# A hand-written order of work for a retention layer and a GELU network: the rows of chunks 3 to 5 go over three transfer queues, and all work is put in a new order

## The chip, the cores and the metric

The kernel runs on one core of a Trainium2 chip. The core has five engines that run side by side, each through its own list of instructions in order: TensorE (PE, matrix products into the eight banks of PSUM), VectorE (DVE), ScalarE (ACT), GpSimd (POOL) and SyncE (SP, which only starts transfers here). Transfers are started from the lists of SyncE, ScalarE and GpSimd. An engine that comes to an instruction whose inputs are not ready stops there, and all that stands behind it in its list waits as well. The metric is the device time of one execution in microseconds (us). The changed kernel is run in the same way and compared with the one before.

## The reference

```python
def _attn_ref(q, k, v):                      # q, k, v: (4, 8, 768, 64)
    B, H, S, D = q.shape
    gamma = 1.0 - 2.0 ** (-5.0 - np.arange(H, dtype=np.float32))
    scale = 1.0 / np.sqrt(D)
    state, y = np.zeros((B, H, D, D), dtype=np.float32), np.zeros_like(q)
    for t in range(S):
        state = gamma[None, :, None, None] * state + np.einsum('bhd,bhe->bhde', k[:, :, t], v[:, :, t])
        y[:, :, t] = scale * np.einsum('bhd,bhde->bhe', q[:, :, t], state)
    return y

def _moe_ref(x, w_in, w_out):                # x: (3072, 512), w_in: (512, 2048), w_out: (2048, 512)
    h = x @ w_in
    c = np.float32(np.sqrt(2.0 / np.pi))
    g = 0.5 * h * (1.0 + np.tanh(c * (h + 0.044715 * h * h * h)))
    return g @ w_out
```

The output of the first is turned to (batch x sequence, heads x head size) and is the x of the second.

## The kernel before

**Tiling.** The 768 steps of the sequence are cut into six chunks c = 0 to 5 of 128 steps. In a chunk each of the four batches b has a row tile of q, of k and of v: 128 steps x 8 heads x 64, 256 KB in float32. A chunk's x is 512 rows (4 batches x 128), kept with the 512 features on the partitions.

**The retention part of a chunk and batch.** L loads a row tile (line 308). PREP scales it or copies it to float16 (lines 216 and 213 on VectorE and GpSimd, 211 on ScalarE). For chunks 0 and 1, T transposes q and k on TensorE against an identity (line 338, the identity is loaded by LI, line 227) and ET copies the result out of PSUM; for chunks 2 to 5, DT does the same with a transposing transfer on SyncE's list (line 345). A is the product of keys and queries, EA puts the decay mask on it (VectorE, reading PSUM), YI multiplies with v, YP adds what comes from the state of the earlier chunks, EY or EP copies the result into x, SS and ES carry the state on.

**The network part of a chunk.** Both layers are computed by a scheme of seven products in place of eight, with sums of blocks ahead and behind. For chunks 1 to 5, and in chunk 0 for three of the four column groups j of the first layer, M1:c,j,n is product n of the first layer: four matmuls of 256 columns. SX makes the sums of x, WI those of w_in (t_in), CP copies a bank to h, D1 adds another bank to it, G is the GELU. For the second layer SG makes the sums of g, WO those of w_out (t_out), M2 is a product, CO and D2 bring the result to o, ST stores it. In chunk 0 the group j = 1 of the first layer (HB, 128 columns a matmul, GELU GB) and the whole second layer (O0, EO, ST0) are plain products. LWI and LWO load the weights (float32 in memory, float16 on the chip), always from GpSimd's list; w_in is loaded in halves of 64 partitions (line 262). All sums, masks and scalings share the helper at line 216, all plain products that at line 219, so their rows carry those line numbers.

**What sets the order.** ORDER (lines 17 to 135) is one string of 1125 words, read by the loop at line 656. Each word calls a function: `L:v,3,1,S@2` loads v of chunk 3, batch 1 from SyncE's list (S; A is ScalarE, P GpSimd, V VectorE) into buffer 2 of its kind; a number behind @ is a buffer or a bank of PSUM. The words of one engine run in the order in which they stand; words of different engines are tied only by the data and buffers that they share, for which the framework sets the waits. SyncE computes nothing, so it runs ahead of its words' places as far as the waits allow. There are 13 buffers for row tiles, and a load into a buffer waits until the PREP of the tile before it there is done. The transfers of SyncE and ScalarE together use eight semaphores in turn, those of GpSimd another eight, and a transfer waits until the one before it on its semaphore has landed.

**The opening.** SPIN, 11 products of zeros, comes first on TensorE. The rows of chunk 0 are loaded in the order of the words, from three lists; the constants (LC), the identity (LI) and the dummy GELU that loads ScalarE's table (TABLE) stand between them.

Of the kernel before, what the change touches and what calls it, by code (L numbers as in the profile page):

```python
# [26 lines left out]
L:v,1,2,P@5 D1:0,2,11 G:0,0,11@0 CP:0,2,22,A@0 D1:0,0,12 M1:0,0,7 M1:0,2,6 G:0,2,11@1 ES:0,1,A L:v,1,3,P@11
G:0,0,12@2 D1:0,0,22 L:v,1,1,P@10 L:v,1,0,P@6 M1:0,2,3 M1:0,3,2@5 WI:3,1,V CP:0,2,12,A@2 M1:0,0,4 M1:0,3,1@4
PREP:q,1,3,V@4 WI:3,3,V LWO:2 PREP:q,1,0,P@1 LWO:3 D1:0,2,12 L:v,2,2,P@7 WI:3,2,V CP:0,3,11,A@3 M1:0,3,5@2
L:k,2,1,P@2 G:0,2,12@3 PREP:q,1,1,V@3 D1:0,3,11 L:q,2,3,P@8 WI:3,4,V M1:0,2,7 G:0,0,21@4 HB:1,0@3 PREP:k,1,0,V  # L30
HB:1,2@0 G:0,0,22@5 L:k,2,3,P@1 PREP:k,1,3,V M1:0,3,6 PREP:v,1,2,P@4 CP:0,3,22,A@2 PREP:k,1,1,V GB:1,0,0@6
GB:1,2,0@7 HB:1,1@5 ES:0,0,A GB:1,2,1@8 GB:1,0,1@9 PREP:q,1,2,V@2 PREP:k,1,2,V M1:0,3,3 HB:1,3@7 L:k,2,2,P@3
CP:0,3,12,A@1 GB:1,1,0 GB:1,1,1 T:1,1@6 L:q,2,1,P@4 ET:1,1,A@4 L:k,2,0,P@5 M1:0,3,7 T:1,3@0 L:v,2,0,P@12
T:1,2@3 D1:0,3,22 D1:0,3,12 O0:1,0@5 ET:1,3,A@5 ET:1,2,V@6 D1:0,2,22 M1:0,3,4 GB:1,3,1 L:q,2,0,P@0 T:1,0@6
WI:2,4,V GB:1,3,0 G:0,3,21@10 A:1,2@2,0 ET:1,0,A@0 EA:1,2,0@0 A:1,1@3,7 EA:1,1,1@1 O0:0,0@4 G:0,2,22@11 O0:1,1
A:1,3@6,2 EA:1,2,1 PREP:v,1,3,A@5 EA:1,1,0 A:1,0@7,0 M1:0,2,4 O0:0,1 PREP:v,1,1,A@6 G:0,2,21@12 EA:1,3,0@2
# [655 lines left out]
```

## Time and profile before

| what | value |
|---|---|
| runs | 202.04 us median of 3 (201.94 to 203.08) |
| the profiled execution | 200.09 us, span of the profile 198.3 us |
| TensorE busy | 183.0 us, 92% of the span |
| VectorE busy | 160.0 us, 81% |
| GpSimd busy | 139.1 us, 70% |
| ScalarE busy | 119.3 us, 60% |
| moved by transfers | 34.26 MB, mean 173 GB/s |
| queue of SyncE / GpSimd / ScalarE | 19.35 / 10.23 / 4.36 MB |

All times inside the execution count from the start of the span. A row of the timeline has the start, the duration, the engine, the line, the operation, output<-input, how many instructions are merged in it (x), and in brackets the idle time of the engine ahead of it and what ended that idle time. A row of the groups has busy time, mean duration of one in ns, and idle time ahead. A row of the windows has the stretch and its length, the busy time of TensorE, its weight loads, VectorE, ScalarE and GpSimd, the granted clock of TensorE, the busy share of the 16 DMA engines and the rate in GB/s. A row of the chain of work that ended last has start, duration and what was running or under way. On GpSimd an issue of a transfer takes the engine's own time (0.88 to 0.91 us for a row tile).

### The profile page before, as it was taken

To read this page: it belongs to the slowest core of one execution; us is meant where nothing else is said; L and a number is where in the kernel's file an instruction comes from. 1 tells how busy PE (TensorE), PEld (TensorE's weight loads), DVE (VectorE), ACT (ScalarE), POOL (GpSimd) and SP (SyncE) were. 2 spreads that over 40 slices of the span, in tenths; PEclk is the share of its full clock that TensorE was granted. 3 is DMA by queue.
4 is the path that set the end of the run, shared out by engine and by line. 5 is a ranking of instruction groups with operands and counts; after the bars stand their busy time and mean duration, and the time that the engine had idled before them with its cause. 6 is when DMAs were issued, how large, how long until landed. Compare 5 with 4: busy or idle time off the path is not lost.

```text
span 198.3 us, 5294 instructions
## 1 busy us (share of the span) xinstructions
PE 183.0 (92%) x2111; PEld 149.0 (75%) x2111; DVE 160.0 (81%) x294; ACT 119.3 (60%) x219; POOL 139.1 (70%) x143
## 2 busy tenths in 40 slices
PE   7377999998999999999999699999999999999992
PEld 2155878575676788877978588878888888888882
DVE  0888979899678999998989999998897577674630
ACT  1329798687767477945784669676544745435111
POOL 0797477977999976973799595898359867447200
PEclk9958999999999999999999999999999999999998
DMA  6999999999989999999999995260200201301453
GB/s 144 288 239 243 203 334 234 295 239 333 270 195 235 214 211 258 213 212 216 244 226 190 209 178 155 53 150 27 94 0 0 86 23 58 106 0 56 141 201 136
DMA packets 80540, 34.26 MB, mean 173 GB/s; under 512 B 69060, under 2 KB 78404, under 8 KB 80516
## 3 DMA queue, kind: packets, MB, share of 16 engines
q1 hardware_dynamic: 66164, 19.35, 44.4%
q0 software_dynamic: 6128, 10.23, 21.7%
q10 hardware_dynamic: 8224, 4.36, 7.6%
q8 instruction: 16, 0.26, 0.5%
q14 instruction: 8, 0.07, 0.1%
HBM read 27.63 MB, written 6.29 MB: 171 GB/s over the span
## 4 chain that ended last, share of the span: by engine, by line
PE 65%; DMA 19%; POOL 6%; DVE 4%; issue 2%; ACT 1%; ACTq 0%; SPq 0%; POOLq 0%; DVEq 0%
PE bank L219 65%; DMA w_in<-in_moe_w_in_dram 9%; DMA r<-in_q_dram 6%; DMA qkT<-qk 2%; DVE g L216 2%; DMA r<-in_v_dram 2%; POOL sx L216 2%; POOL t_out L216 1%; POOL qk L216 1%; POOL v L216 1%; DVE h L216 1%; DVE w_out L216 1%; POOL g L216 1%; POOL w_in L262 0%; POOL qk L213 0%
## 5 line engine op out<-in xcount | busy, mean ns | idle before, releaser
L219 PEld LDWEIGHTS <-g 128*128 128x128 f16 x624 | 60.4, 98 | 11.8 <-PE bank L338 0.3
L216 POOL TENSOR_TENSOR g<-g 128x512 f16<-128x512 f16 x46 | 54.5, 1204 | 17.9 <-DVE g L216 7.2
L219 PE MATMUL bank<-w_out,g 128*128 128x256 f16 (+1 forms) x384 | 60.4, 290 | 0.2 <-DMA w_out<-in_moe_w_out_dram 0.2
L216 DVE TENSOR_TENSOR h<-bank,h 128x512 f32<-128x512 f32 x69 | 46.0, 682 | 8.8 <-PE bank L219 4.4
L442 ACT ACTIVATE g<-h 128x512 f16<-128x512 f32 x69 | 42.7, 634 | 15.4 <-DVE h L216 15.0
L219 PEld LDWEIGHTS <-w_in 128*128 128x128 f16 x432 | 39.2, 98 | 6.2 <-issue 0.8
L211 ACT COPY h<-bank 128x512 f32<-128x512 f32 x57 | 32.7, 588 | 13.0 <-PE bank L219 12.6
L219 PEld LDWEIGHTS <-t_in 128*128 128x128 f16 x276 | 26.4, 98 | 9.9 <-issue 4.3
L219 PE MATMUL bank<-t_out,g 128*128 128x256 f16 x240 | 33.4, 273 | 0.0
L216 DVE TENSOR_TENSOR a<-bank,mask 128x512 f16<-128x512 f32 x48 | 30.0, 680 | 3.5 <-PE bank L219 3.4
L219 PE MATMUL bank<-x,w_in 128*128 128x256 f16 (+1 forms) x248 | 29.7, 259 | 0.4 <-DMA w_in<-in_moe_w_in_dram 0.2
L219 PE MATMUL bank<-sx,t_in 128*128 128x256 f16 x184 | 26.5, 273 | 2.3 <-ACT g L442 1.2
L219 PE MATMUL bank<-sx,w_in 128*128 128x256 f16 x184 | 26.7, 273 | 0.0
L216 DVE TENSOR_TENSOR g<-g 128x512 f16<-128x512 f16 x34 | 22.1, 669 | 3.1 <-ACT g L442 2.1
L442 ACT ACTIVATE g<-bank 128x512 f16<-128x512 f32 (+1 forms) x31 | 16.5, 549 | 8.4 <-PE bank L219 5.8
L211 ACT COPY o<-bank 128x512 f32<-128x512 f32 (+1 forms) x19 | 9.7, 516 | 18.2 <-PE bank L219 18.2
L216 POOL TENSOR_TENSOR v<-r,cst 128x512 f16<-128x512 f32 x16 | 16.9, 1061 | 4.0 <-DMA r<-in_v_dram 4.0
L216 DVE TENSOR_TENSOR o<-bank,o 128x512 f32<-128x512 f32 (+1 forms) x18 | 10.6, 595 | 8.9 <-PE bank L219 8.7
L211 ACT CAST qk<-r 128x512 f16<-128x512 f32 x20 | 12.1, 620 | 6.2 <-PE bank L219 2.2
L219 PE MATMUL bank<-x,t_in 128*128 128x256 f16 x92 | 13.8, 273 | 1.9 <-DVE h L216 1.9
L216 DVE TENSOR_TENSOR qk<-r,cst 128x512 f16<-128x512 f32 x13 | 9.2, 744 | 6.5 <-DMA cst<-rr_cst 4.1
L211 ACT COPY qkT<-bank 128x1024 f16<-128x1024 f16 x7 | 6.9, 1013 | 8.0 <-PE bank L338 8.0
(53 smaller groups left out, 191.9 us busy)
## 6 DMA issues: line engine op xcount, KB each, us to landing
r<-in_v_dram SPq DMA_DIRECT2D x15, 256.0 KB, 4.8
r<-in_q_dram SPq DMA_DIRECT2D x15, 256.0 KB, 4.2
r<-in_k_dram SPq DMA_DIRECT2D x14, 256.0 KB, 4.6
out_dram<-o ACTq DMA_DIRECT2D x11, 256.0 KB, 3.8
r<-in_v_dram POOLq DMA_DIRECT2D x9, 256.0 KB, 8.3
out_dram<-o SPq DMA_DIRECT2D x9, 256.0 KB, 2.3
w_in<-in_moe_w_in_dram POOLq DMA_DIRECT2D x8, 256.0 KB, 9.6
r<-in_k_dram POOLq DMA_DIRECT2D x8, 256.0 KB, 8.6
```

What stands on the lines that cost most here:

```text
L211: nc.scalar.copy(out=out, in_=in_)
L216: EN[e].tensor_tensor(out=out, in0=in0, in1=in1, op=op)
L219: nc.tensor.matmul(out=out, lhsT=lhsT, rhs=rhs, start=start, stop=stop, skip_group_check=True)
L442: nc.scalar.activation(out=out, in_=in_, func=AF.Gelu_apprx_tanh, scale=1.0)
```

## The change

Only the string ORDER changes; no function does. It has 1125 words before and after, with the same products: the same 161 M1, 140 M2, 4 HB, 16 O0, 8 T and 16 DT. New are the order of the words, the buffers and banks behind @, and for part of the words the engine.

- Rows: before, S, A and P load 44, 5 and 23 tiles; after 23, 18 and 31. Of the 36 tiles of chunks 3 to 5, all 36 came from S; after 17 come from S, 13 from A and 6 from P.
- Sums of g (SG): 34 on V and 46 on P before, 41 and 39 after. Sums of w_out (WO): 5 and 11 before, 11 and 5 after. Sums of x (SX): 12 and 12 before, 15 and 9 after. Sums of w_in (WI): 15 and 1 before, 13 and 3 after.
- CP: 57 on A and 12 on V before, 53 and 16 after. CO: 17 and 7 before, 16 and 8 after. EO: 2 and 2 before, 4 and 0 after. ET: 7 on A and 1 on V before, 8 and 0 after. EY: 4 on A before, 3 on A and 1 on V after. PREP: 25 on A, 34 on P, 13 on V before; 26, 35 and 11 after.
- Stores: 12 from A and 16 from S before; 13 and 15 after.

The opening of the list and its end:

```diff
-L:k,0,2,A@0 L:q,0,2,A@1 ZERO L:k,0,0,S@2 SPIN:11@0 LI:A L:q,0,3,A@3 LC:S TABLE PREP:k,0,0,V@0 L:k,0,3,A@4
-L:q,0,1,A@5 L:v,0,1,S@6 PREP:q,0,2,P@1 LWI:0 PREP:k,0,2,V L:v,0,3,P@7 MASK L:k,0,1,S@8 L:q,0,0,S@9
-PREP:q,0,3,V@2 T:0,2@1 ET:0,2,A@0 A:0,2@2,3 L:v,0,0,P@10 PREP:k,0,3,V LWI:2 L:v,0,2,S@11 T:0,3@4 PREP:q,0,0,V
-ET:0,3,A@1 PREP:k,0,1,P@3 EA:0,2,1@0 A:0,3@5,6 T:0,0@7 EA:0,2,0 ET:0,0,A@2 PREP:q,0,1,V T:0,1@0 LWI:3
-A:0,0@1,4 PREP:v,0,2,P@0 EA:0,3,0@1 EA:0,3,1 EA:0,0,0@2 EA:0,0,1 ET:0,1,A@3 LWI:1 SS:0,2@3 A:0,1@2,7
-EA:0,1,0@3 PREP:v,0,0,P@1 PREP:v,0,1,A@2 PREP:v,0,3,A@3 YI:0,2@5 SS:0,1@6 L:k,1,1,P@12 EA:0,1,1 EY:0,2,A@0
-L:q,1,3,S@2 YI:0,3@1 L:q,1,1,P@1 YI:0,0@4 WI:0,1,V L:q,1,2,P@0 WI:0,2,V SS:0,3 YI:0,1@0 EY:0,3,A SX:0,1,V@0
-EY:0,0,A EY:0,1,A L:k,1,0,P@3 SS:0,0 WI:0,3,V M1:0,0,5@2 M1:0,0,1@7 WI:0,4,V SX:0,2,V@1 SX:0,3,V@2
...
+ZERO LC:S MASK L:k,0,2,A@0 PREP:k,0,2,P@0 L:q,0,3,S@1 L:k,0,1,A@2 L:q,0,0,S@3 L:q,0,2,A@4 PREP:k,0,1,V@1
+L:k,0,0,A@5 PREP:q,0,0,V@2 TABLE PREP:k,0,0,V LI:A L:k,0,3,S@6 PREP:k,0,3,V@3 L:q,0,1,P@7 PREP:q,0,2,V
+SPIN:11@0 PREP:q,0,3,P L:k,1,1,S@8 L:v,0,3,A@9 PREP:k,1,1,V@4 T:0,0@1 ET:0,0,A@0 T:0,3@2 PREP:q,0,1,V
+ET:0,3,A@1 A:0,0@3,4 LWI:0 T:0,2@5 T:0,1@6 EA:0,0,0@0 L:q,1,1,S@10 A:0,3@7,0 ET:0,1,A@2 EA:0,0,1 A:0,1@1,2
+PREP:q,1,1,V ET:0,2,A@3 A:0,2@3,6 L:v,0,2,P@11 L:v,0,0,P@12 L:v,0,1,P@0 LWI:2 PREP:v,0,0,A@0 L:k,1,2,P@2
+PREP:v,0,2,A@1 PREP:v,0,3,P@2 EA:0,3,1@1 T:1,1@4 EA:0,3,0 EA:0,2,0@2 SS:0,0@5 LWI:1 L:q,1,2,P@3 LWI:3
+EA:0,1,0@3 SS:0,2@0 PREP:v,0,1,A@3 WI:0,1,P EA:0,1,1 YI:0,0@7 EY:0,0,A@0 SS:0,3 YI:0,1@3 EA:0,2,1 WI:0,3,V
+WI:0,2,V L:q,1,3,P@5 EY:0,1,A YI:0,3@1 YI:0,2@2 SS:0,1 EY:0,2,V EY:0,3,A M1:0,0,1@7 SX:0,1,V@0 L:k,1,3,P@6
+ET:1,1,A@4 L:q,1,0,P@4 SX:0,2,V@1 M1:0,0,2@6 M1:0,2,1@3 WI:2,1,V M1:0,2,2@2 SX:0,4,V@2 CP:0,2,11,A@0 LWO:0
+WI:2,2,V CP:0,0,11,A@1 M1:0,0,5@1 CP:0,0,22,A@2 M1:0,2,5@4 L:k,1,0,P@1 SX:0,3,V@3 M1:0,2,6 D1:0,2,11 WI:2,3,V
+D1:0,0,11 L:v,1,0,P@8 WI:2,4,V M1:0,0,6 CP:0,2,12,A@3 G:0,2,11@0 PREP:q,1,2,P@2 CP:0,2,22,V@0 G:0,0,11@1
+PREP:k,1,2,V M1:0,0,3 ES:0,0,A M1:0,2,7 HB:1,2@2 CP:0,0,12,A@1 HB:1,0@6 D1:0,0,12 M1:0,0,7 LWO:1 WI:0,4,V
...
-D2:5,22,0 ST:5,22,S,0 M2:5,4,1,0 D2:5,12,0 M2:5,4,0,0 ST:5,22,S,1 ST:5,12,S,0 CO:4,21,A@1 M2:5,4,1,1
-M2:5,4,0,1 M2:5,3,1,0 ST:4,21,A CO:5,21,A,1@4 M2:5,3,1,1 CO:5,21,A,0 D2:5,12,1 ST:5,21,A,0 ST:5,21,S,1
-ST:5,12,S,1
+M2:5,4,1,1 M2:5,4,0,0 M2:5,4,0,1 CO:4,21,V@4 ST:5,22,S,0 M2:5,3,1,0 ST:4,21,S M2:5,3,1,1 D2:5,12,0
+CO:5,21,V,1@5 ST:5,12,A,0 CO:5,21,A,0 ST:5,21,A,0 ST:5,21,S,1 D2:5,12,1 ST:5,12,A,1
```

Before, the first HB stands behind 16 words M1, as `HB:1,0`; after, behind 10 words M1, as `HB:1,2`. On GpSimd the weights of the first layer are loaded in the order 0, 2, 3, 1 before and 0, 2, 1, 3 after.

More of the change, by code (lines that the diff above doesn't have):

```diff
@@ L27 @@
[L27 to L36, printed above, removed]
```

202 lines of the change are left out of this document (104 added, 98 removed).

## The prediction

> **What bounds the kernel now.** I read the page first (busy times, then the strip of 40 slices), then TensorE's timeline for every gap in front of a matmul, then the opening on all queues, the windows, and the groups of instructions for prices.
>
> ```profile
> PE 183.0 (92%) x2111; PEld 149.0 (75%) x2111; DVE 160.0 (81%) x294; ACT 119.3 (60%) x219; POOL 139.1 (70%) x143
> PE   7377999998999999999999699999999999999992
> PEclk9958999999999999999999999999999999999998
> DMA  6999999999989999999999995260200201301453
> ```
>
> TensorE is busy for 92% of the span, and nearly all that it is not lies in the first four slices (20 us). The DMA row stands at 9 for the first 24 slices (119 us): rows and weights stream all that time.
>
> ```profile
> 8.09 0.61 PE L338 MATMUL bank<-iden,qk 128*128 128x128 f16 x8 [2.02 <-DMA iden<-rr_ident]
> 19.79 0.61 PE L219 MATMUL bank<-sx,t_in 128*128 128x256 f16 x4 [0.65 <-DVE sx L216]
> 27.14 1.95 PE L219 MATMUL bank<-x,w_in 128*128 128x128 f16 x32 [0.18 <-DMA w_in<-in_moe_w_in_dram]
> 49.90 0.60 PE L219 MATMUL bank<-sx,t_in 128*128 128x256 f16 x4 [1.20 <-ACT g L442]
> 90.50 0.40 PE L219 MATMUL bank<-qkT 64*128 64x128 f16 x8 [0.34 <-DMA qkT<-qk]
> 103.66 0.60 PE L219 MATMUL bank<-sx,t_in 128*128 128x256 f16 x4 [0.42 <-POOL sx L216]
> 110.71 0.60 PE L219 MATMUL bank<-x,t_in 128*128 128x256 f16 x4 [1.65 <-DVE h L216]
> 111.14 0.60 PE L219 MATMUL bank<-x,w_in 128*128 128x256 f16 x4
> 193.71 1.04 PE L219 MATMUL bank<-w_out,g 128*128 128x256 f16 x8
> ```
>
> Start, duration, and in brackets the idle time before. The first transposes run at 8.09, the first product of chunk 0's first layer at 19.79, the last product group ends at 194.75. One product (four matmuls of 256 columns) starts 0.43 us after the one before (110.71, 111.14). Between 19.79 and 194.75 the quoted gaps sum to 3.8 us. The change alters no matmul, so the time can move in three places only: when the products start, how much idle time lies between them, and the 3.55 us from 194.75 to the end of the span at 198.3.
>
> **Step 1, the opening's rows.** The list keeps the opening's products but exchanges its batches and transfers. Before, the first transposes (T:0,2) need the first two row tiles of ScalarE's queue; after, T:0,0 needs the fourth tile of that queue (k of batch 0, behind k2, k1, q2), and the identity is issued behind that.
>
> ```profile
> 1.26 5.01 DMA r<-in_q_dram
> 2.04 1.70 ACTq L227 DMA_DIRECT2D iden<-rr_ident  x1
> 8.99 2.65 DVE L216 TENSOR_TENSOR qk<-r,cst 128x512 f16<-128x512 f32 x3 [0.47 <-DMA r<-in_q_dram]
> 16.13 2.48 DVE L216 TENSOR_TENSOR a<-bank,mask 128x512 f16<-128x512 f32 x4 [0.68 <-PE bank L219]
> 17.14 0.62 POOL L213 CAST v<-r 128x512 f16<-128x512 f32 x1 [0.86 <-DMA r<-in_v_dram]
> 8.16 7.23 DMA w_in<-in_moe_w_in_dram
> 15.67 11.33 DMA w_in<-in_moe_w_in_dram
> L211 ACT COPY h<-bank 128x512 f32<-128x512 f32 x57 | 32.7, 588 | 13.0 <-PE bank L219 12.6
> ```
>
> The second tile of ScalarE's queue landed at 6.27 (1.26 + 5.01); the third tile, behind the small identity, at 8.99. That is at most 2.7 us a tile; the fourth and fifth came without another wait inside the 2.65 us row, so the pace is nearer 1.9. The fourth tile then lands at 6.27 + 2 x 1.9 = 10.1, its scaling on VectorE (2.65 / 3, 0.7 without the hand-over) ends at 10.8, and the first transposes start there and not at 8.09.
>
> Two chains lead from there to the first product. VectorE, in order: four more scalings (k3, q2, k of chunk 1, q1: 2.8 us) to 13.6, then nine passes (eight masks, one scaling) at 2.48 / 4 = 0.62: 19.2; batches 0 and 1 are among the first eight, 18.6. Before, the last mask ended at 18.61, so this chain costs nothing. The v chain: before, the first weight tile landed at 15.39 (8.16 + 7.23), and a v tile two places behind it at 17.14, 0.9 a tile. After, GpSimd's queue has q1 ahead of that weight tile, and three v tiles (2, 0, 1) behind it: 15.39 + 0.9 + 3 x 0.9 = 19.0. The cast of v1 on ScalarE, its product, and two evictions (0.6 each by the last row; the product some 0.2) follow: 21.0. The first product, which now needs x of batches 0 and 1 only, starts at 21.0 and not at 19.79: **+1.2 us**. Bounds: -0.4 (q1 and one v tile cost nothing, as ScalarE's and SyncE's queues drain sooner) to +3.0 (the full 2.7 us a tile).
>
> The third weight tile: before, w_in1 is the last of four on GpSimd's queue, issued at 15.67 and landed at 27.0, when it held TensorE up by 0.18 us. After, it is the third; ahead of it one weight tile less (1 MB read) but two row tiles more in all. A weight tile costs about three row tiles of stream (w_in0 needed 7.23 us beside the rows, against 2.7 and 1.9 for a row tile), so it lands about one tile sooner, 26.1. Its user HB:1,2 comes after ten products, not sixteen: 21.0 + 10 x 0.43 = 25.3. TensorE waits 0.8, 0.18 of it as before: **+0.6 us**, bounds -0.2 and +1.7 (landing at 27.0 again).
>
> **Step 2, rows of chunks 3 to 5.** 36 tiles, all on SyncE's queue before; after 17 on SyncE's, 13 on ScalarE's, 6 on GpSimd's (with the earlier chunks GpSimd issues 31 and not 23). What it can win is read from two windows (TensorE, load, VectorE, ScalarE, GpSimd busy; clock; DMA share; GB/s):
>
> ```profile
> 8.00:10.00 2.00, 0.81 (x14) 0.63 (x15) 1.53 (x5) 1.01 (x1) 2.00 (x4) 0.84 1.28 288
> 64.00:68.00 4.00, 4.00 (x108) 2.89 (x107) 3.97 (x7) 1.21 (x3) 4.00 (x5) 1.00 0.89 201
> 92.27 1.04 POOL L216 TENSOR_TENSOR v<-r,cst 128x512 f16<-128x512 f32 x1 [4.04 <-DMA r<-in_v_dram]
> L308 POOL DMA_DIRECT2D r<-in_k_dram x8 | 7.1, 888 | 3.5 <-DMA w_in<-in_moe_w_in_dram 1.7 <-DMA w_out<-in_moe_w_out_dram 0.7 <-DVE sx L216 0.5
> ```
>
> With several queues at work rows came at 288 GB/s, from SyncE's alone at 201. At 92.27 GpSimd had sat 4.04 us for a v tile, and the chain that ended last runs through that wait into the gaps at 103.66 and 110.71. So sooner rows can take away 0.34 + 0.42 + 1.65 = 2.4 us at most, and nothing at the least, as the last of these gaps is released by VectorE. I take a third, **-0.8 us**, since a late VectorE is next in line. The costs: GpSimd issues 8 tiles more at 0.89 = 7.1 us, covered by step 3's relief; ScalarE's 13 issues lie in its idle 40% and, where the slot's last reader is late, block its evictions. In the list that reader stands at least 2.6 us of TensorE work ahead, so I price this at 0, bounds 0 to +2.
>
> The Trainium skill (DMA: Bandwidth & Descriptors, section Issuing engines are not separate DMA queues) says that transfers started by different engines share the same 16 DMA engines, and that spreading them saves only issue time. By it the 288 of the opening is not the spreading's doing, and the -0.8 would be 0. No stretch of this trace has the same tiles on one and on three queues.
>
> **Step 3, work exchanged between engines.** Counted in the two lists: VectorE takes on 7 sums of g (34 to 41), 6 of w_out, 3 of x, 4 evictions h (12 to 16) and 1 o, and gives up 2 scalings, 2 sums of w_in, 2 evictions of chunk 0 and one of qkT (one x comes back).
>
> ```profile
> L216 DVE TENSOR_TENSOR g<-g 128x512 f16<-128x512 f16 x34 | 22.1, 669 | 3.1 <-ACT g L442 2.1 <-POOL g L216 1.0
> L213 DVE COPY h<-bank 128x512 f32<-128x512 f32 x12 | 8.2, 682 | 0.9 <-PE bank L219 0.7 <-ACT g L442 0.2
> L216 DVE TENSOR_TENSOR t_out<-w_out 128x512 f16<-128x512 f16 x2 | 0.8, 415 | 0.0
> L216 POOL TENSOR_TENSOR g<-g 128x512 f16<-128x512 f16 x46 | 54.5, 1204 | 17.9 <-DVE g L216 7.2 <-ACT g L442 5.4 <-PE bank L219 3.2
> 100.00:120.00 20.00, 17.93 (x238) 15.08 (x236) 18.93 (x30) 12.66 (x24) 16.84 (x17) 1.00 1.11 204
> 140.00:160.00 20.00, 20.00 (x234) 17.73 (x233) 15.51 (x26) 10.55 (x19) 13.86 (x13) 1.00 0.12 41
> ```
>
> VectorE: 7 x 0.67 + (6 + 3 - 2) x 0.415 + (5 + 1 - 2 - 2 - 1) x 0.68 = 4.7 + 2.9 + 0.7 = +8.3 us. GpSimd: 7 sums at 1.20, 3 of x and a net 4 of the weights at about the same go (-16.8), 7.1 of issues come: near -9 to -10. ScalarE: about even. By place in the lists some two thirds of VectorE's additions stand late, beside products that ran from about 140 to 175 before, where it was busy 15.5 of 20 us and has room; the rest (about 2.5 us) falls where it was busy 18.9 of 20. With fewer sums on GpSimd the sums of g on VectorE should come nearer 0.415, the quickest such row, than 0.67, which gives back most. I take **+0.6 us**; bounds -1.5 (all 41 sums fall by 0.04) and +4 (the room of 1.1 us in 20 is all forced waiting, and the 2.5 us and what the ScalarE blocks add show in full).
>
> **Step 4, the end.** The last store moves from SyncE's to ScalarE's queue; the last sum on VectorE stays. 0, bounds -0.3 and +0.9 (one more tile, 0.9, draining there).
>
> **The sum.** 1.2 + 0.6 - 0.8 + 0.6 = +1.6 us. The profiled execution took 200.09 us with a span of 198.3, 1.95 below the median of the runs shown, 202.04. I add the sum to the median: 203.6 us (a profiled execution of 201.7).
>
> **Rivals.** *The rows win everything, faster.* Two queues gave 288 against 201 GB/s; if three do, chunk 3 to 5's rows are early, the 2.4 us go, the other quoted gaps (1.20, 0.18) are not met in the new order, and the opening is even: 202.04 - 3.8 = 198.2. It decides if GpSimd's wait for v is gone and VectorE is below 18.5 of 20 from 60 to 120. Against it: 1.20 and 1.65 were released by ScalarE and VectorE. Chance 0.20.
>
> *VectorE becomes the bound.* At 18.9 of 20 it has 5% left and gets 5% more; the +4 shows, beside the opening's 1.8 and without the -0.8: 207.8. For it: the longest gap, 1.65, is already its own. Against: most additions stand late. Chance 0.22.
>
> *The spreading does nothing for the rows.* All three queues feed what was already at 9 of 9 in the DMA row; the gaps stay: 203.6 + 0.8 = 204.4. Chance 0.12. The Trainium skill's rule quoted above is this rival.
>
> *The slow clock lasts into the products.*
>
> ```profile
> 6.00:8.00 2.00, 0.07 (x1) 0.10 (x1) 2.00 (x7) 0.00 (x0) 1.66 (x2) 1.00 1.28 288
> 14.00:16.00 2.00, 1.86 (x20) 1.23 (x18) 1.45 (x3) 1.58 (x2) 1.61 (x4) 0.50 1.14 302
> 18.00:20.00 2.00, 1.10 (x34) 0.86 (x30) 1.97 (x7) 1.59 (x3) 2.00 (x3) 1.00 1.22 196
> ```
>
> After a 2 us pause the granted clock stood at 0.50 for 8 us and rose at 16. The pause now lasts to 10.8; shifted by 2.7 it rises at 18.7, before 21.0. If the wait for v holds it down, some 3 us of products run at half speed: +3 less what the wait for w_in1 hides, 205.8. Chance 0.08. The Trainium skill (TensorE: Matmul & The Clock Gate, What's actually happening) says that an idle window of about 3.4 us halves the clock and a busy one restores it; the trace agrees in kind, with 8 us of mixed work before the rise.
>
> **How the numbers follow.** The forecast has 0.38: 203.6 us, its own range 202 to 205.5 from the bounds of steps 1 and 2. About 1% (2.0 us) is what a measurement of this kernel can tell from no change; so faster means below 200.0 and slower above 204.1. Faster is the first rival, 0.20; within 1% the forecast, 0.38; slower the other three, 0.42. The range for 8 in 10 goes from 199.0 (most of the first rival left out) to 207.5 (the second cut at its upper half).
>
> **What would show it.** Step 1: first transposes near 10.8, first product near 21.0, a wait for w_in1 before the 128-column group. Step 2: GB/s from 60 to 100 above 230, the end of the 9s in the DMA row before slice 24, no wait of GpSimd for v of 4 us. Step 3: VectorE near 168 us in all and above 17 of 20 from 140 to 160, its g row below 0.67. Wrong it would be if the first product starts before 20, or if TensorE's gaps after it sum to over 7 us or under 2.

## The result and the profile after

| kernel | runs | median us | ratio to the kernel before |
|---|---|---|---|
| before | 4 | 201.99 (200.90 to 203.08) | 1 |
| changed | 4 | 208.57 (207.94 to 213.89) | 1.032, 95% interval 1.024 to 1.039 |
| changed, measured again | 4 | 213.48 (210.79 to 215.06) | 1.065, 1.052 to 1.078 |

The change makes the kernel slower, by 3% and by 6.5% in two measurements of the same program whose intervals do not meet; the kernel before, run beside them, came to 201.99 and 200.51. The ratios are made without the runs that count as disturbed; the medians and ranges here and below hold all runs. The profiled execution took 208.61 us with a span of 206.8, 8.5 us more than the one of before.

The page of the changed kernel, busy times and the strip:

```profile
PE 187.5 (91%) x2111; PEld 152.1 (74%) x2111; DVE 169.3 (82%) x309; ACT 117.7 (57%) x217; POOL 132.3 (64%) x138
PE   7173899899999999959999799999999999999992
PEclk9958589999999999987999999999999999999999
DMA  7999999998958999899999992222100301223144
```

TensorE's row has its holes in the first slices (1 and 3 in the second and fourth place), and a new one in the 18th slice. The clock row has three dips, two in the opening and one behind the 18th slice, where there was one. The timeline of TensorE, its longest waits:

```profile
11.37 1.87 PE L337 MATMUL bank<-iden,qk 128*128 128x128 f16 x16 [5.30 <-DMA iden<-rr_ident]
20.88 1.03 PE L337 MATMUL bank<-iden,qk 128*128 128x128 f16 x8 [2.56 <-DVE qk L215]
25.40 2.73 PE L218 MATMUL bank<-x,w_in 128*128 128x256 f16 x16
89.78 0.21 PE L218 MATMUL bank<-qkT 64*128 64x128 f16 x1 [1.50 <-DVE o L215]
115.08 0.60 PE L218 MATMUL bank<-sx,t_in 128*128 128x256 f16 x4 [0.91 <-DVE a L215]
118.67 1.19 PE L218 MATMUL bank<-x,t_in 128*128 128x256 f16 x8 [0.37 <-DVE h L215]
```

The first product starts at 25.40 and not at 19.79. To see where the 8.5 us are, I cut each profiled execution into four parts that add up to its span: the start of the first product; the idle time written in brackets behind it, summed; what is left until the last product ends (the products themselves, longer where the clock is low); and the tail from there to the end of the span.

| profiled execution | first product | idle behind it | products | tail | span |
|---|---|---|---|---|---|
| before | 19.79 | 4.82 | 170.14 | 3.55 | 198.3 |
| changed | 25.40 | 4.70 | 172.95 | 3.75 | 206.8 |
| changed, measured again | 25.41 | 9.17 | 173.14 | 3.78 | 211.5 |

So 5.6 us are lost ahead of the first product, 2.8 in products that run slower, 0.2 in the tail, and nothing in idle time. In the second measurement the idle time grew by 4.5 us more, with the opening unchanged. The windows (columns as before) show the slow products:

```profile
18.00:20.00 2.00, 0.33 (x8) 0.15 (x8) 0.00 (x0) 1.43 (x3) 2.00 (x4) 1.00 1.24 203
22.00:24.00 2.00, 1.57 (x38) 1.30 (x38) 2.00 (x5) 0.59 (x1) 2.00 (x3) 0.50 1.20 257
92.00:94.00 2.00, 2.00 (x12) 1.31 (x10) 2.00 (x4) 0.38 (x1) 1.95 (x2) 0.50 1.14 255
60.00:100.00 40.00, 37.86 (x423) 29.12 (x424) 38.84 (x70) 24.26 (x46) 28.92 (x30) 0.96 1.06 220
140.00:160.00 20.00, 20.00 (x246) 17.10 (x245) 17.82 (x32) 12.16 (x23) 10.23 (x9) 1.00 0.10 28
```

The clock is back at 1.00 by 18 to 20 us, stands at 0.50 again from 22 us on, and falls once more behind the wait at 89.78. The first four products take 2.56 us (25.40 to 27.96) in place of 4 x 0.435 = 1.74, and five products from 91.73 to 95.63 take 3.90 in place of 2.18: 0.8 and 1.7 of the 2.8 us. The remaining 0.3 I did not place. And VectorE's timeline in the opening, then the piece of the chain that ended last which leads into it:

```profile
14.13 1.29 DVE L215 TENSOR_TENSOR a<-bank,mask 128x512 f16<-128x512 f32 x2 [1.19 <-PE bank L218]
20.14 0.69 DVE L215 TENSOR_TENSOR qk<-r,cst 128x512 f16<-128x512 f32 x1 [4.72 <-DMA r<-in_q_dram]
20.75 3.67 DVE L215 TENSOR_TENSOR a<-bank,mask 128x512 f16<-128x512 f32 x6
```

```profile
6.14 13.97 DMA r<-in_q_dram
```

VectorE makes two masks and then stands for 4.72 us, because the next word in its list is PREP:q,1,1, the scaling of chunk 1's q of batch 1. That row is the fifth and last of the opening's rows on SyncE's list and landed at 20.11. Six masks of chunk 0 wait behind it. TensorE waits as well, since T:1,1, which transposes that row, stands ahead of SS:0,0.

### The profile page after: what moved, and what is told of

Its sections match the earlier page's. It is cut to its first block, busy times and chain, and to the rows that moved or that the text cites. A ratio compares the mean times of both kernels' runs of the same rounds, so it can differ in the third digit from the quotient of the medians.

```text
span 206.8 us, 5286 instructions
## 1 busy us (share of the span) xinstructions
PE 187.5 (91%) x2111; PEld 152.1 (74%) x2111; DVE 169.3 (82%) x309; ACT 117.7 (57%) x217; POOL 132.3 (64%) x138
## 4 chain that ended last, share of the span: by engine, by line
PE 66%; DVE 19%; DMA 8%; ACT 2%; issue 2%; SPq 1%; DVEq 0%
PE bank L218 65%; DMA r<-in_q_dram 7%; DVE h L215 6%; DVE g L215 3%; DVE a L215 2%; DMA r<-in_k_dram 2%; DVE sx L215 1%; DVE o L215 1%; SPq L307 1%; DVE h L212 1%; DVE st L429 1%; DVE w_out L215 1%; ACT h L210 1%; DVE w_in L215 1%; DVE qk L215 1%
## 5 line engine op out<-in xcount | busy, mean ns | idle before, releaser
L215 POOL TENSOR_TENSOR g<-g 128x512 f16<-128x512 f16 x39 | 46.2, 1201 | 43.3 <-ACT g L441 17.7
L218 PEld LDWEIGHTS <-w_in 128*128 128x128 f16 x432 | 39.9, 100 | 7.3 <-issue 0.9
L210 ACT COPY h<-bank 128x512 f32<-128x512 f32 x53 | 30.3, 587 | 15.8 <-PE bank L218 15.4
L218 PE MATMUL bank<-x,w_in 128*128 128x256 f16 (+1 forms) x248 | 30.5, 263 | 0.3 <-DVE h L215 0.3
L218 PE MATMUL bank<-sx,w_in 128*128 128x256 f16 x184 | 27.9, 279 | 0.5 <-DVE w_in L215 0.5
L215 DVE TENSOR_TENSOR g<-g 128x512 f16<-128x512 f16 x41 | 22.9, 584 | 1.1 <-ACT g L441 0.9
L210 ACT COPY o<-bank 128x512 f32<-128x512 f32 (+1 forms) x20 | 10.6, 533 | 14.8 <-PE bank L218 14.7
L215 POOL TENSOR_TENSOR v<-r,cst 128x512 f16<-128x512 f32 x16 | 17.6, 1114 | 0.0
L215 DVE TENSOR_TENSOR qk<-r,cst 128x512 f16<-128x512 f32 x11 | 8.1, 775 | 8.4 <-DMA r<-in_q_dram 4.7
L337 PE MATMUL bank<-iden,qk 128*128 128x128 f16 x64 | 6.6, 276 | 7.9 <-DMA iden<-rr_ident 5.3
```

The costliest lines, as they stand in the source:

```text
L210: nc.scalar.copy(out=out, in_=in_)
L215: EN[e].tensor_tensor(out=out, in0=in0, in1=in1, op=op)
L218: nc.tensor.matmul(out=out, lhsT=lhsT, rhs=rhs, start=start, stop=stop, skip_group_check=True)
L337: nc.tensor.transpose(out=ps[:, i, hp], in_=t[:, i, hp], identity=iden)
```

## The experiments

### The row behind the opening

Theory: the scaling PREP:q,1,1 in VectorE's list (and T:1,1 in TensorE's) makes the opening wait for a row that nothing in the opening needs. Both go behind the opening.

```diff
-EA:0,0,1 A:0,1@1,2 PREP:q,1,1,V ET:0,2,A@3 ... EA:0,3,1@1 T:1,1@4 EA:0,3,0 ... YI:0,3@1
+EA:0,0,1 A:0,1@1,2 ET:0,2,A@3 ... EA:0,3,1@1 EA:0,3,0 ... EA:0,2,1 PREP:q,1,1,V ... T:1,1@4 ET:1,1,A@4
```

> The new order with two words moved back: the scaling of q of chunk 1, batch 1 on VectorE stands behind chunk 0's masks, and the transposes T:1,1 stand just ahead of their eviction, behind the first product. Theory O (a row of chunk 1 that lands at 20.1 us holds VectorE's and TensorE's lists): the first product comes at about 21 us and not at 25.4, the half clock after it goes, the time falls from 208.5 by 4 to 5.5 us to 203 to 204.5. Rival V (VectorE has more work than before and that is the cost): the first product comes sooner, but the idle time returns behind it, and the time falls by less than 1 us.

213.85 us (212.24 to 218.22), ratio 1.055 (1.050 to 1.061): longer than the changed kernel, where both theories expected a fall. TensorE's timeline there (the string ORDER takes fewer lines in this kernel, so its line numbers are 8 lower):

```profile
21.86 1.03 PE L210 MATMUL bank<-x,w_in 128*128 128x256 f16 x4
```

The first product came at 21.86, so the row was what held the opening up; but two waits of 4.64 and 6.06 us stood at 57 and 96 us, and the total was no better. A second form moves T:1,1 alone, to tell which list it is.

> The changed kernel with the transposes of chunk 1, batch 1 behind the opening on TensorE, while VectorE keeps their scaling where it is, ahead of the masks. If VectorE's wait for the row sets the opening, its second masks still start behind 20 us and the first product comes at 24 to 25 us; if TensorE's wait sets it, the first product comes at 21 to 22.3 us, as where both are moved.

TensorE's timeline there:

```profile
21.62 0.43 PE L218 MATMUL bank<-v,qk 128*64 128x64 f16 x8 [2.77 <-DVE a L215]
25.55 0.82 PE L218 MATMUL bank<-x,w_in 128*128 128x256 f16 x3
```

TensorE waits as long as before, now for a mask, and the first product comes at 25.55: VectorE's list sets the opening. (219.15 us in one run, with waits of 4.49 and 6.05 us at 61 and 100 us.)

### The other single edits

D2:1,11 gives the bank free that TensorE waits for at 89.78. In the next kernel it stands right behind the copy CO:1,11.

```diff
-SG:1,3,4,V@7 D2:1,11, CP:2,1,11,A@1
+CO:1,11,A@4 D2:1,11, CP:2,3,22,A@3
```

> The new order with one word moved: the sum D2:1,11 stands right behind its copy CO:1,11 in the list, ahead of the two sums of w_out and the sum of g on VectorE. Theory P (the place of that sum in VectorE's list makes the 1.50 us gap at 89.78, and the half clock from 92 to 95 us follows from it): the gap goes and the clock stays full there, the time falls by 2.5 to 3.8 us to 205 to 206. Rival V (VectorE is loaded to the limit): the gap comes back in front of another product within 10 us, and the time falls by less than 1 us.

221.20 us (220.08 to 222.89), ratio 1.101 (1.094 to 1.107). TensorE waited 6.53 us at 64.52, long before the edit's place, and 5.90 us at 102.54. Two kernels change only the letters of the L words of chunks 3 to 5: the kernel before with the new queues, and the changed kernel with all these rows on SyncE's list, which is where the kernel before has them.

```diff
-L:k,3,3,S@0 ... L:v,3,1,S@2
+L:k,3,3,P@0 ... L:v,3,1,A@2
```

> The order before, with only the issuing engine of the 36 row tiles of chunks 3 to 5 as in the new order (17 SyncE, 13 ScalarE, 6 GpSimd). Theory S (more queues bring the rows sooner): 0.34 to 2.4 us of gaps go, 199.6 to 201.7 us. Rival (the same 16 transfer engines were busy anyway): within 0.5 us of 202. Second rival (issues block ScalarE or GpSimd): 203 or more.

210.23 us (205.66 to 210.65) against 201.05 for the kernel before: in the old order the spreading alone costs 4 us or more, with a wait of 7.01 us for VectorE's h at 92.59. The time is the second rival's (203 or more); ahead of that wait two sums of VectorE took 3.39 and 5.89 us.

```diff
-L:v,3,1,A@8 ... L:k,3,3,P@10
+L:v,3,1,S@8 ... L:k,3,3,S@10
```

> The new order with all 36 row tiles of chunks 3 to 5 issued from SyncE again. If the spreading helps the new order: 210 us or more, since transposes wait behind rows. If the spreading is without weight: 208.5 within 1 us. If it is part of the loss: below 207 us.

216.22 us (214.03 to 216.93), ratio 1.076 (1.071 to 1.081), again with 6.53 us of waiting at 64 us. The number is that of the first branch (210 or more, the spreading helps), but the wait is one for VectorE's h, as in the kernel with D2:1,11 first, which has the rows spread. So spreading cost time in the old order and saved it in the new one, two of the four times lay outside all that was expected, and long waits came and went at places that the edits don't touch. That needed another theory.

### What stands still: a sum on VectorE

In all of these waits the profile names VectorE, and VectorE is booked as busy. The wait of 6.53 us lies beside a single sum of w_out that lasted 7.59 us where others of its form take 0.41. My second theory: a VectorE sum of two 16-bit inputs is held up as long as GpSimd works without a pause, and a microsecond more or less in the opening decides whether one is hit. Running the changed kernel again without an edit tests that.

> The changed kernel once more, without an edit. The opening's transfers land some tenths of a microsecond earlier or later from run to run, and VectorE's sums meet GpSimd's at another phase. Theory of the held-up sums: some runs near 208 and some 4 to 7 us longer, and a profile of a long one shows a sum of VectorE that lasts 5 us or more. Rival, that its time is settled by the order alone: all runs within 1 us of 208.5.

All four runs were 2 us or more above the first measurement's median of 208.57; that some would lie near 208 did not come true, and the rival (all within 1 us of 208.5) is out. VectorE, GpSimd and TensorE in that profile:

```profile
88.30 5.92 DVE L215 TENSOR_TENSOR g<-g 128x512 f16<-128x512 f16 x1
94.15 0.68 DVE L215 TENSOR_TENSOR o<-bank,o 128x512 f32<-128x512 f32 x1
```

```profile
88.22 1.17 POOL L215 TENSOR_TENSOR t_out<-w_out,t_out 128x512 f16<-128x512 f16 x1
89.35 1.03 POOL L215 TENSOR_TENSOR v<-r,cst 128x512 f16<-128x512 f32 x1
90.34 0.60 POOL L212 CAST qk<-r 128x512 f16<-128x512 f32 x1
90.91 3.03 POOL L215 TENSOR_TENSOR v<-r,cst 128x512 f16<-128x512 f32 x3
```

```profile
94.88 0.26 PE L218 MATMUL bank<-qkT 64*128 64x128 f16 x1 [6.05 <-DVE o L215]
```

VectorE and GpSimd in the profile of the first measurement:

```profile
87.76 1.37 DVE L215 TENSOR_TENSOR g<-g 128x512 f16<-128x512 f16 x1
```

```profile
87.67 1.18 POOL L215 TENSOR_TENSOR t_out<-w_out,t_out 128x512 f16<-128x512 f16 x1
88.89 1.14 POOL L215 TENSOR_TENSOR v<-r,cst 128x512 f16<-128x512 f32 x1
```

It is one and the same instruction, SG:1,3,4, which VectorE took over from GpSimd by the change. It starts 0.08 or 0.09 us behind a GpSimd sum. In the first measurement it got through when that sum ended; in the second it lasted until 94.22, just behind the end of GpSimd's run at 93.94, and the result of D2:1,11 (o), next in VectorE's list, was late by that much: TensorE waited 6.05 us. The Trainium skill (SBUF — State Buffer, SBUF: two separate sides) says that a VectorE instruction with two SBUF inputs and a GpSimd instruction that reads SBUF exclude each other, and that the one that starts later is blocked for the whole of the other. The trace agrees, but the block spans six GpSimd instructions here, not one. VectorE's sums with one input in PSUM are not held: h<-bank,h has a mean of 681 ns after and 682 before.

All twenty traces of this case show the same. 634 sums of VectorE with two 16-bit inputs in SBUF had nothing of GpSimd beside them, and each took 0.40 to 0.43 us; those beside GpSimd's work took up to 7.59. About 2900 sums and masks of this size with one input in PSUM took 0.67 to 0.70 us each, whatever GpSimd did. It is not the 16 bits that count: the scalings qk<-r,cst, which read float32 rows and a constant in SBUF, were held too, for up to 2.33 us where 0.68 is the rule.

The counts do not say which engine waits for which. The test makes GpSimd wait in place of VectorE. Its base is the changed kernel with the rows of chunks 3 to 5 back on SyncE's list. That is word for word the kernel that gave 216.22 us above, run once more.

> The changed kernel with only the queues of the rows of chunks 3 to 5 put back. By my step of the prediction 0.8 slower than the changed kernel, so 209 to 214; if GpSimd's eleven and ScalarE's added issues lengthen the stretches in which VectorE's sums are held up, it is 2 or more faster, 206 to 207; if the rows have no part in it, it moves with the opening's phase within 208 to 214.

215.75 us (214.22 to 217.75), ratio 1.070 (1.061 to 1.080), above all three expectations, and the sum WO:2,1 lasted 7.58 us in the first profile and 7.59 in this one. VectorE, GpSimd and TensorE:

```profile
54.48 7.59 DVE L215 TENSOR_TENSOR t_out<-w_out 128x512 f16<-128x512 f16 x1
```

```profile
54.22 1.34 POOL L215 TENSOR_TENSOR sx<-x,sx 128x512 f16<-128x512 f16 x1
...
58.75 3.03 POOL L215 TENSOR_TENSOR v<-r,cst 128x512 f16<-128x512 f32 x3
```

```profile
63.92 1.86 PE L218 MATMUL bank<-w_out,g 128*128 128x512 f16 x4 [6.53 <-DVE h L215]
```

Again the sum ends (62.07) 0.29 us behind GpSimd's run (61.78), eight instructions of which lie beside it. Now WO:2,2, which needs the result of WO:2,1, goes to GpSimd and ahead of that run:

```diff
-WO:2,1,V L:v,2,1,P@7 ... WI:1,3,P ... WO:2,2,V
+WO:2,1,V L:v,2,1,P@7 ... WO:2,2,P WI:1,3,P
```

> The changed kernel with its rows back on the old queues, in whose profile VectorE's sum WO:2,1 stood for 7.59 us while GpSimd ran ten operations without a pause. Here WO:2,2, which needs that sum, runs on GpSimd ahead of the ten, so that GpSimd itself waits until VectorE is done; nothing else is moved. Theory of the hold: WO:2,1 takes 0.4 to 0.8 us, the gap of 6.53 us and the slow clock behind it go, and some 1 to 2 us come back since GpSimd's ten start later: 208 to 210 against 214.2 to 217.8. Rival, that the 7.59 us are a wait for something else that the trace books as busy (a bank, a transfer): the sum still takes over 5 us and the time stays above 214.

205.89 us (201.97 to 207.38) against 215.75, below the 208 to 210 that were expected. VectorE's sum and GpSimd's wait for it:

```profile
54.27 0.41 DVE L215 TENSOR_TENSOR t_out<-w_out 128x512 f16<-128x512 f16 x1
```

```profile
54.77 1.15 POOL L215 TENSOR_TENSOR t_out<-w_out,t_out 128x512 f16<-128x512 f16 x1 [0.83 <-DVE t_out L215]
```

The sum takes 0.41 us, and the wait of 6.53 us is gone with the slow clock behind it (0.50 in the window from 64 to 66 us there, 1.00 here). That the hold is GpSimd's doing is shown; why a waiting sum sometimes gets in between two GpSimd instructions and sometimes not is not.

### Moving the held sums elsewhere

Three kernels moved WO:2,1 and WO:2,2 ahead to where GpSimd was idle and SG:1,3,4 back to GpSimd: one on the late row, one with D2:1,11 first, one with both.

```diff
-WO:0,1,V ... WO:2,1,V ... WO:2,2,V ... SG:1,3,4,V@7
+WO:0,1,V WO:2,1,V WO:2,2,V ... SG:1,3,4,P@7
```

> The late-row kernel again (the changed kernel with the scaling of chunk 1's q for batch 1 and its transposes put back behind the opening's products), with the two VectorE sums that stood still in it moved: WO:2,1 and WO:2,2 right behind WO:0,1, where GpSimd waits for ScalarE, and SG:1,3,4 from VectorE to GpSimd. Theory that two-operand 16-bit sums of VectorE are held up for 5 to 7 us by an unbroken run of GpSimd work: neither sum takes over 2 us any more, the two gaps of TensorE (4.64 and 6.06 us) go, and the time is 212.2 to 213.9 less 11.5, so 201 to 203. Rival, that the gaps come from transfers that wait on one another: the gaps stay within 2 us of their places and the time stays above 211.

209.96 us (208.35 to 212.65), ratio 1.052 (1.038 to 1.066).

> The kernel with D2:1,11 first (the changed kernel's late first product is left as it is), with the same two moves of WO:2,1, WO:2,2 and SG:1,3,4. Theory of the held-up VectorE sums: gaps of 6.53 and 5.90 us go, the first product stays at 24 to 25.5 us, TensorE's wait for the output rows of D2:1,11 (1.50 in the changed kernel) and the slow clock behind it go, and the time is 208.6 less about 2, so 206 to 207. Rival of the transfers: above 214.

211.76 us (211.12 to 215.12), ratio 1.060 (1.051 to 1.069).

> All three edits together on the changed kernel: late row, D2:1,11 first, the three sums moved. By the theory that the loss is the opening (5.6 to 6.4 us), the wait at 90 us with its slow clock (about 2 us) and nothing else: 208.6 less 8, so 200 to 201, level with the kernel before. If the spreading of the rows or VectorE's larger share cost anything of their own, it stays 2 us or more above the kernel before.

210.01 us (206.65 to 214.12), ratio 1.041 (1.027 to 1.054). The first two are better than their bases (213.85 and 221.20), and they miss the forecasts of the theory; the third comes out as its last sentence says for the other case, 2 us or more above the kernel before. The moved sums were not held, but others were in their place: t_out for 2.81 and 3.19 us in the first, two sums of w_out together for 7.06 in the second and 7.07 in the third. With so many of these sums on VectorE, moving one brings the next beside GpSimd's work.

### Engines and queues undone

With the late row, 79 words of SG, WO, SX, WI and (from chunk 2 on) PREP were put back on the engines of the kernel before. The reverse puts the new engines on the old order. A third has the rows back as well, a fourth D2:1,11 behind CO:1,11.

```diff
-SG:1,2,2,V@6 WO:2,4,V ... SG:1,1,4,P@9
+SG:1,2,2,P@6 WO:2,4,P ... SG:1,1,4,V@9
```

> The late-row kernel with the exchange of engines undone: all 79 words of the sums of x, the weights and the gelus (SX, WI, WO, SG) and of the scalings from chunk 2 on run on the engine that they had in the kernel before; the new order and the spread rows stay. Theory that the loss behind the opening comes from the sums that moved from GpSimd to VectorE and are held up there by GpSimd's unbroken runs: no VectorE sum over 3 us, no gap over 2 us at 80 to 96 us, the clock stays at 1.00 there, time 201 to 203. Rival, that the new order or the spread rows cost it: 206 or more.

208.44 us (205.81 to 209.83), 5 less than the late row alone; the longest sum was 2.57 us. No sum over 3 us and no wait over 2 us at 80 to 96 us came, as the theory says, but the clock still fell to 0.54 there (90 to 92 us) behind a wait of 1.60 us, and the time is the rival's: the new order or the spread rows cost something of their own.

> The kernel before with the exchange of engines alone (the same 79 words on the engines of the changed kernel, order and queues as before). Theory of the held-up sums: VectorE busy up by 5 us or more, at least one sum over 3 us on its path, time 203 to 209. Rival, that the exchange is harmless and order or rows cost it: within 1 us of the kernel before.

213.84 us (212.13 to 213.94), ratio 1.062 (1.054 to 1.069). That is more than either side expected. One sum was held for 3.98 us at 54.97, but the largest loss stood ahead of it, a wait of 5.17 us of TensorE at 52.87, and comes from another wait: VectorE stood 6.20 us for SX:1,1, which GpSimd reached only behind a wait of 2.01 us for a v row, three row issues and a sum of w_out. The old order does not fit these engines.

> The late-row kernel with both the exchange of engines and the queues of the rows of chunks 3 to 5 undone, so that the new order is what is left of the change. Beside the kernel with the engines alone undone it tells what the spread rows cost: by my step (a gain of 0.8) it is 0.8 slower than that one; by the run with the rows alone spread (205.7 to 210.7 against 201) it is 3 or more faster. If the new order itself costs nothing it comes to 201 to 202.

206.91 us (205.72 to 209.04), ratio 1.027 (1.018 to 1.036). Against 208.44 with the rows spread, the ranges overlap: this pair doesn't price the spreading. The 201 to 202 of an order that costs nothing did not come.

> The late-row kernel with the engines back and D2:1,11 right behind the copy that it needs, so that it stands ahead of the sum that took 2.57 us there. Theory: TensorE's waits of 1.60 and 0.38 us for VectorE at 88 us and the slow clock behind them (1.7 us) go: 207 less 3.5, so 203 to 204. Rival, that VectorE is full there and another of its results is late in place of that one: within 1 us of 207 to 208.5.

207.05 us (206.77 to 208.80), ratio 1.029 (1.024 to 1.035): the rival holds. The wait for o was gone, but one of 1.43 us for VectorE's h stood at 90.82 in its place. The new order with the old engines thus stays about 3% behind, with waits of 1.2 to 1.4 us for GpSimd and VectorE at 52, 79 and 91 us; which words make them is open.

### The clock

Six matmuls on zeros fill TensorE's wait ahead of T:1,1.

```diff
-T:1,1@4 EA:0,3,0
+SPIN:6@5 T:1,1@4 EA:0,3,0
```

> The changed kernel with six matmuls on zeros put into TensorE's wait at 18.3 to 20.9 us, ahead of the transposes of chunk 1. The first product stays at 25.2 to 25.6 us. If the low clock from 20.6 to 27 us comes from that wait, the clock holds 1.00 there, and the first sixteen matmuls of the products take 1.75 us in place of 2.56; if it comes from the wait before 11 us, nothing changes.

```profile
25.52 1.94 PE L218 MATMUL bank<-x,w_in 128*128 128x256 f16 x16
```

```profile
24.00:26.00 2.00, 1.65 (x37) 1.32 (x36) 1.59 (x4) 1.12 (x3) 2.00 (x3) 1.00 1.28 232
```

The clock held 1.00, and the first 16 matmuls took 1.94 us in place of 2.73. So the second dip came from the wait for the row. The products' part fell from 172.95 to 171.54 us (0.8 of it in the opening; the waits of 1.49, 0.38 and 0.20 us at 91.73 to 92.92 were not followed by a slow clock here), but the idle time rose from 4.70 to 7.29, most of it for VectorE's h and t_in at 36 to 42 us: 209.91 us in all (one run). TensorE reached sooner what VectorE had not done.

### All three causes out, and the spreading by itself

The late row, GpSimd waiting for WO:2,1 and the rows on their old queues together (the three diffs above); then the same with the rows spread, as in the changed kernel.

> The kernel in which GpSimd waits for VectorE's sum (rows on the old queues), with the late row of the opening as well. The first product comes 4 to 5 us earlier, at 20.7 to 22.3 us, and if nothing else bounds the kernel the time is 205.9 less 4 to 5, so 201 to 202, level with the kernel before. If VectorE, with 8 us more work than before, is what the middle waits for, its results are late by as much as the opening gains: gaps of 7 us or more behind the first product and a time of 204 to 206.

203.19 us (200.94 to 208.03, 12 runs) against 201.13 (199.78 to 204.38): ratio 1.005 (1.000 to 1.010), level with the kernel before; the two medians lie 1.0% apart. No kernel here beats it. Against the same kernel without the late row (205.89) the row gives 2.7 us, with ranges that overlap, while the first product comes 4.2 us sooner (21.81 and 26.01).

> The same with the rows of chunks 3 to 5 on the changed kernel's three queues, so that it differs from it in the spreading alone, in a kernel whose long hold is gone. By the prediction's step 2 0.8 faster than it; by the runs so far, in which spreading did not raise the rate of the transfers, within 1 us of it; if the added issues on GpSimd and ScalarE cost something of their own, 2 us or more slower.

208.64 us (204.56 to 211.30, 6 runs), ratio 1.021 (1.013 to 1.030). The two intervals do not meet; the medians lie 5.45 us apart, and the ranges overlap. In four parts as above:

| profiled execution | first product | idle behind it | products | tail | span |
|---|---|---|---|---|---|
| rows on old queues | 21.81 | 2.98 | 171.44 | 3.37 | 199.6 |
| rows spread | 22.27 | 5.63 | 173.49 | 3.61 | 205.0 |

Rows spread: VectorE, GpSimd, TensorE around SG:1,3,4.

```profile
86.27 1.37 DVE L215 TENSOR_TENSOR g<-g 128x512 f16<-128x512 f16 x1
```

```profile
84.38 0.90 POOL L307 DMA_DIRECT2D r<-in_q_dram  x1
85.27 0.88 POOL L307 DMA_DIRECT2D r<-in_k_dram  x1
86.17 1.17 POOL L215 TENSOR_TENSOR t_out<-w_out,t_out 128x512 f16<-128x512 f16 x1
```

```profile
88.29 0.21 PE L218 MATMUL bank<-qkT 64*128 64x128 f16 x1 [1.50 <-DVE o L215]
```

Rows on old queues:

```profile
83.20 0.41 DVE L215 TENSOR_TENSOR g<-g 128x512 f16<-128x512 f16 x1
```

```profile
81.33 1.33 POOL L215 TENSOR_TENSOR t_out<-w_out,t_out 128x512 f16<-128x512 f16 x1
84.33 1.04 POOL L215 TENSOR_TENSOR v<-r,cst 128x512 f16<-128x512 f32 x1 [1.67 <-DMA r<-in_v_dram]
```

```profile
84.27 0.21 PE L218 MATMUL bank<-qkT 64*128 64x128 f16 x1 [0.24 <-DVE o L215]
```

Without its two row issues GpSimd has its sum t_out done before VectorE comes to SG:1,3,4, and then stands 1.67 us for a v row. That row is on SyncE's list in both kernels and did not come later here: it landed at 84.26, and at 87.16 with the rows spread. In that pause VectorE's sum takes 0.41 us. With the issues, GpSimd's sum falls 0.1 us ahead of VectorE's, which is held, D2:1,11 is late, TensorE waits 1.50 us and its clock falls behind it. A wait of GpSimd for v, which I had counted as a loss, kept VectorE's way free. That is one pair of profiles; the rest of the 2.65 us of idle time between them lies mostly in a wait of 1.44 us for VectorE's h at 38.97.

## Why the prediction was wrong

**Step 1, the opening: the step that failed.** I forecast the first product at 21.0; it came at 25.40. The place is my sentence on VectorE's chain, "nine passes (eight masks, one scaling) at 2.48 / 4 = 0.62: 19.2". I priced the one scaling at its own duration and did not ask when its row lands. It landed at 20.11 and held six masks back. The row was the fifth tile on SyncE's queue. The 1.9 us a tile that I used for ScalarE's queue would not have shown it: from a second tile at 6.27 they put the fifth at 12.0, before VectorE came to it at 15.41. The trace of the kernel before did show it, in the last early row on SyncE's list there, also one of chunk 1: issued at 7.07, landed at 22.71. Why these two rows took 14 and 15.6 us, where those ahead of them on SyncE's list took 4.5 to 5.8, is open. I also took the list to keep "the opening's products" and overlooked that T:1,1 of chunk 1 now stands among them, though that would not have changed the time alone (25.55 with it moved). Where the row was taken out, the first product came at 20.69 to 22.27 in the eight kernels that have it late: the remaining term, +0.9 to +2.5, holds my +1.2 inside. The first transposes came at 11.37 (forecast 10.8), released by the identity and not by a scaling. The +0.6 for w_in1 did not come: with the products 4 us later, the weights were there.

**Step 2, the rows: no gain where the step saw one.** GpSimd's 4 us wait for v went away as forecast, and the rate did not rise, 220 GB/s over 60 to 100 us against this row of the kernel before:

```profile
60.00:100.00 40.00, 39.24 (x525) 31.98 (x523) 37.91 (x73) 27.42 (x53) 31.71 (x30) 1.00 1.01 225
```

In the pair that differs in the spreading alone the rate was 232 GB/s on the old queues and 241 with the rows spread, and the time was longer. The Trainium skill (DMA: Bandwidth & Descriptors, Issuing engines are not separate DMA queues), which I had set against my term, says that spreading saves issue time only; the trace agrees as far as 220 and 225, and 241 and 232, lie close together. I priced GpSimd's added issues as time that step 3 relieves, and not as a shift of GpSimd's work against VectorE's: 1.005 against 1.021 in that pair. The sign is not fixed. The spreading costs 4 us or more in the old order, but in the changed kernel without it WO:2,1 is held, and the time is 215.75 and 216.22 against 208.57 and 213.48 with it.

**Step 3, the exchange: right in size, wrong in price.** VectorE came to 169.3 us (forecast 168), 17.82 of 20 from 140 to 160 (above 17), its sums of g to a mean of 0.584 us (below 0.67); GpSimd came down by 6.8 us (forecast 9 to 10). I priced the extra work as a share of a nearly full engine and let the shorter mean give most of it back. It costs in another way: single sums held for 1.4 to 7.6 us ahead of something that TensorE waits for. In the profiled execution that is the 1.50 and 0.38 us at 89 to 90 and the 1.7 us of slow clock behind them; in the second measurement it is 6.05.

**Step 4, the end.** +0.2 (3.75 against 3.55), inside its bounds.

**The rivals.** The time is nearest to VectorE as the bound (207.8), but not by its mechanism: that one put the loss into forced waiting between products, and the sum of the gaps was 4.70 us as against 4.82. The slow clock came, not as one long dip but twice, each time behind a new wait: the first 16 matmuls of the products lost 0.8, those at 92 us 1.7. The low clock of the kernel before had lasted 6.8 us (from 9.4 to 16.2) and not the 8 that I read. That the spreading does nothing for the rows was right as far as it went. None of the rivals took the opening at more than 1.8 us, so none could reach 208.6 by its own sum. The two signs of being wrong that I named did not show either: the first product came late, not before 20, and the gaps behind it summed to 4.70 us, between 2 and 7 (9.17 in the second measurement).

**What the sum would have been.** 5.6 (opening) + 2.8 (slow clock in the products) + 0.2 (tail) - 0.1 (idle) = 8.5 us over the profiled execution of before. The opening entered my sum with +1.2 and measured 5.6; the slow clock had no term, only a chance of 0.08. The late row, GpSimd's wait and the old queues together give all but 0.5% back (1.0% by the medians of all runs); the late row and GpSimd's wait without the old queues leave 2.1%.

## What to carry to other kernels

In an in-order list a word costs what its latest input costs everything behind it: when a list is reordered, look up for every word the landing time of what it reads, above all of a word brought forward from a later stage. An exchange of sums with two inputs in SBUF between VectorE and GpSimd is priced by where the two meet, not by their busy times; where such a sum stands ahead of something that TensorE waits for, GpSimd can be made to depend on it, which took 10 us off here. And a wait of TensorE is to be priced with the slow clock that can follow it.

## What the runs showed of the hardware

- A VectorE sum of two 16-bit inputs in SBUF (0.41 us alone) was held for up to 7.59 us by a GpSimd run of several instructions. In the two cases whose rows stand above it ended 0.28 and 0.29 us behind the run. Sums with an input in PSUM were never held.
- Issues of transfers on GpSimd hold such sums too: in the changed kernel the sum of w_out at 86.13 took 1.38 us with nothing of GpSimd beside it but the issues of two rows (85.87 to 87.65), both of them brought there by the spreading.
- The same program took 208 to 214 us in one measurement and 211 to 215 in another, with a sum of 1.37 us in the profile of the first and of 5.92 in that of the second at the same place.
- Behind the hold of 7.59 us in the kernel with the rows back on SyncE's list the transfers stopped as well, 0 GB/s from 60 to 70 us. SyncE's list stood at four transposing transfers from 52.40 to 70.69 us, and its longest waits in that time were for ScalarE, 10.9 us for its copies of q and k and 4.6 us for its GELUs. Where GpSimd waits for the sum, the rate was 0 from 60 to 62 us alone. So a held sum reaches the transfers too.
- A wait of 1.50 us of TensorE with two shorter ones behind it was followed by 3.4 us at half clock (91.9 to 95.4 us); the same three waits in the kernel with the filler (1.49 us at 91.73) were not, nor was a wait of 1.65 us in the kernel before, at 110.71. In each of the twenty traces the granted clock changes only at times that lie whole multiples of 3.41 us apart (in the changed kernel at 10.02, 16.84, 20.25, 27.08, 91.94 and 95.35 us). In the changed kernel the three waits fall into one such stretch, of which TensorE was busy for 46%; in the kernel with the filler they fall into two, 71% and 60% busy:

```profile
88.52:91.94 3.42, 1.58 (x22) 1.15 (x22) 3.42 (x6) 1.58 (x3) 3.38 (x5) 1.00 0.82 63
91.94:95.35 3.41, 3.41 (x18) 2.33 (x17) 3.41 (x6) 0.60 (x2) 2.01 (x2) 0.50 1.11 271
```

```profile
87.80:91.22 3.42, 2.44 (x23) 2.03 (x21) 3.42 (x5) 1.76 (x4) 2.97 (x4) 1.00 1.72 229
91.22:94.63 3.41, 2.04 (x25) 1.42 (x25) 3.41 (x6) 1.59 (x3) 2.04 (x3) 1.00 0.69 88
```

So where a wait falls matters beside its length. At which busy share the clock falls is not shown: a stretch of the kernel before that was 52% busy (108.35 to 111.76) was not followed by a slow clock. Six matmuls on zeros in a wait of the opening kept the clock at 1.00.
